# A transformer block's forward and backward on one core: the opening written out in order on all engines, with the first two head pairs run together

## The chip, the cores and the metric

The kernel runs on one core of a Trainium2 chip. The metric is the device time of one execution in microseconds; several runs of each kernel are made, and their median is given. The engines are named as in the profile: PE is TensorE, PEld its weight loads, DVE is VectorE, ACT is ScalarE, POOL is GpSimd and SP is SyncE, which issues DMAs.

## The reference: what is computed

A block with adaptive layer norms is computed together with its gradients. One row `c` gives six modulation rows through `silu(c) @ w_mod`; `sa, ca, ga` belong to the attention, `sb, cb, gb` to the MLP.

```python
h = _layernorm(x, axis=-1) * (1 + ca) + sa
x = x + ga * _A_ref(h, A_wqkv, A_wo)      # 32 heads of 16, softmax over all 2048 tokens
h = _layernorm(x, axis=-1) * (1 + cb) + sb
x = x + gb * _B_ref(h, B_w1, B_b1, B_w2, B_b2)   # relu(h @ w1 + b1)**2 @ w2 + b2
```

The sizes are 2048 tokens, width 512, MLP width 1792, all in bf16. The ten outputs are the block's result and the gradients of `A_x`, `A_wqkv`, `A_wo`, `w1`, `b1`, `w2`, `b2`, `c` and `w_mod` for a given `grad_out`.

## The kernel before

The program has a forward pass (`phase_fwd`, L265), a backward pass through the attention (`phase5`) and a last phase of weight gradients (`phase6`, L1392). Only the forward pass is touched.

**The attention loop (L331 to L375).** Heads are taken in quads of four (`g`, eight of them) and pairs (`jp`), queries in chunks of 512 (`qc`, four). A head pair of one query chunk is one turn `n` of the outer loop, 64 in all; in each turn the inner loop goes over the 16 key blocks `kb` of 128 tokens. One such step is called a unit. In a unit TensorE makes the scores of two heads (L349, two matmuls of 512 columns into one of two `st` banks; `QTm[j]` holds the queries of one head, with zeros in the rows of the others), ScalarE takes the exponential (L352, `pu`), and TensorE multiplies older `pu` tiles with the values (L314, eight matmuls of 17 columns, called PV). After the last key block VectorE normalises (L321, L322).

**What runs beside it.** While the first query chunk runs, a background generator (`gen_qkv`, L545) hands out single matmuls at a rate of 1.2 per unit: `gen_fm` (L519) projects Q or K of a quad for 512 tokens with four matmuls into a bank `pps` (two banks, shared by all of the opening), evicts them with VectorE (L535), stores them with SP (L536), and makes the token-major copy that the backward pass needs: a DMA transpose on SP (L538, `ev_tm`, three buffers), a copy (L540) and a store (L542) on GpSimd. From quad 3 on it also scales the weights (`wm_s`, L565) and pads the values (`vpad`, L583, L584) on GpSimd, for transposes that the backward pass needs. `load_q` (L293) fetches the queries of the next pair through GpSimd's queue half a pair ahead.

**The opening (`gen_open`, L389).** It loads `x`, the modulation weights and the projection weights through SP, computes the modulation columns (`silu_c`, `mod_cols`), and then, for each chunk of 512 tokens, the layer norm (`norm`: bn_stats and aggregates on VectorE, the power -0.5 on GpSimd, L443, the scaled rows `xhat` on VectorE or ScalarE), 16 transposes on TensorE (`turn`), the modulation into `xm1T` (L466 on VectorE and L469 on ScalarE, one each from the same bank), the K projection of quad 0, and the four value tiles (`values`, evicted in turn by VectorE and ScalarE, L479). The first chunk is done ahead of the loop, with the Q projection of quad 0, whose rows ScalarE copies out of PSUM (L531). Twenty matmuls on constants (L422, L430) keep TensorE busy meanwhile. The other three chunks are handed out piece by piece during the 16 units of head pair 0 (L356 to L361).

**What sets the order.** Under `tc.manual_schedule(engines={PE, SP})` (L160) TensorE and SP run in written order through the forward and backward pass. VectorE, ScalarE and GpSimd are ordered by a scheduler at build time, which may move an instruction ahead of others that were written earlier. [...]

Of the kernel before, what the change touches and what calls it, by code (L numbers as in the profile page):

```python
# [19 lines left out]
P = 128  # L20
DH = 16
EPS = 1e-5

# [81 lines left out]
class K:  # L105
# [71 lines left out]
    def phase0(self):  # L177
# [6 lines left out]
        nc.vector.tensor_copy(self.ident_f[:], self.ident[:])  # L184
# [80 lines left out]
    def phase_fwd(self):  # L265
# [21 lines left out]
        QTm = []  # L287
        for j in range(4):
            t = fw.tile([P, 512], BF16, name=f"QTm{j}")
            nc.vector.memset(t[:], 0.0)  # L290
            QTm.append(t)
# [36 lines left out]
        first = self.gen_open(Vaug, KT, QTm, stp)  # L328
        next(first)
        opening = [9 + DT + DT * 4] * (SC - 1) + [4 * DT + 1]  # L330
        for n, (qc, g, jp) in enumerate(order):  # L331
            if (qc, g, jp) == (1, 0, 0):
                bg.drain()
                self.close_qkv()
                self.open_mlp()
                bg.add(self.gen_weights())
# [3 lines left out]
            for kb in range(ST):  # L340
# [15 lines left out]
                if n == 0:  # L356
                    left = opening[kb // 4]
                    take = -(-left // (4 - kb % 4))
                    opening[kb // 4] -= take
                    for _ in range(take):  # L360
                        next(first)  # L361
                rate = (1.14 if qc else 1.2) if n or kb > 11 else 0
                room = int((SPAN - 2 - bg.plan(rate)) / PVT)
                while pend:
                    age = now - (pend[0][0][0] * ST + pend[0][0][4])
# [4 lines left out]
                if rate:  # L370
                    bg.step(rate)
# [17 lines left out]
    def gen_open(self, Vaug, KT, QTm, stp):  # L389
# [28 lines left out]
        nc.sync.dma_start(self.wmod[:, :, 2 * D:6 * D], wmod_v[:, :, 2 * D:6 * D])  # L418
        self.silu_c(ps)
        warm = ps.tile([P, 512], F32, name="pps")  # L420
        for _ in range(10):
            nc.tensor.matmul(warm[:], lhsT=self.ones_b[:], rhs=QTm[0][:], start=True, stop=True)  # L422
        for t in (1, 0):
            nc.vector.memset(self.wpad0[t][:], 0.0)
        nc.vector.memset(Vaug[:, :, :, DH:DH + 1], 1.0)
        nc.scalar.memzero(wpads[1][:])
        self.mod_cols(ps, (0, 1))
        warm = ps.tile([P, 512], F32, name="pps")
        for _ in range(10):
            nc.tensor.matmul(warm[:], lhsT=self.ones_b[:], rhs=QTm[0][:], start=True, stop=True)  # L430
# [55 lines left out]
        for k2 in range(0, DT, 2):  # L486
            for _ in turn(0, k2):
                pass
# [1156 lines left out]
```

## Time and profile before

| what | value |
|---|---|
| median of 7 runs | 2647.68 us (2635.89 to 2655.86) |
| profiled execution, its own time | 2647.97 us |
| its span | 2646.2 us |
| first exponential of the attention (L352) starts | 24.77 us |
| exponentials of head pair 0 | 24.77 to 61.9 us, 16 units |
| PE busy up to 65.2 us | 48.64 us |
| ACT busy up to 65.2 us | 36.69 us |
| DVE busy up to 65.2 us | 37.05 us |
| end of the forward attention | about 998 us |

In the rows of a timeline the columns are start and duration in us, the engine, the line, the operation, output and input tiles with sizes, the count of instructions merged into the row, and, in brackets, how long the engine had been idle and what released it. In rows of waits they are who waited for whom, the sum in us, how often, and the longest. In rows by stage they are the window, its length, busy us of each engine with its number of instructions, the granted clock of TensorE as a share of full speed (PEclk), the busy share of the DMA engines, and GB/s.

### The profile page before, as it was taken

How to read it: one execution, taken by the hardware profiler on the slowest of the kernel's cores; microseconds unless marked ns; L12 is line 12 of the kernel's file. 1: busy time of each engine (PE TensorE's matmuls, PEld its weight loads, DVE VectorE, ACT ScalarE, POOL GpSimd, SP SyncE). 2: the span in 40 equal slices, each digit the busy share in tenths (PEclk: the TensorE clock that was granted, in tenths of full speed). 3: DMA queues.
4: the chain of work that ended last, by engine and by line, in shares of the span. 5: the costliest groups of instructions: out<-in, count | busy, mean ns of one | idle time of the engine just before them, and what ended most of it. 6: DMA issues, size and time to landing. Idle time of an engine off the chain costs nothing. (4 is left out here: it accounts for less than half of the span.)

```text
span 2646.2 us, 76655 instructions
## 1 busy us (share of the span) xinstructions
PE 2484.4 (94%) x31000; PEld 1230.4 (46%) x31231; DVE 1767.1 (67%) x3653; ACT 2297.9 (87%) x3712; POOL 410.5 (16%) x678
## 2 busy tenths in 40 slices
PE   7999999999999999899999999999999999999997
PEld 3555555555555554753444444444444444443443
DVE  5222223423323344659999999999999999999867
ACT  5999999999999995318999999999999999999733
POOL 3344521310221131350000000000000000000041
PEclk9999999999999999899999999999999999999999
DMA  5488652440441245999999999999999999999986
GB/s 168 99 165 192 171 104 85 117 94 23 131 119 45 88 96 150 209 240 181 202 199 202 205 198 196 199 200 202 198 201 198 202 201 200 200 197 207 197 228 162
DMA packets 1197811, 441.16 MB, mean 167 GB/s; under 512 B 1134958, under 2 KB 1159024, under 8 KB 1197456
## 3 DMA queue, kind: packets, MB, share of 16 engines
q1 hardware_dynamic: 1167584, 347.42, 71.7%
q0 software_dynamic: 29872, 88.83, 11.5%
q8 instruction: 244, 4.00, 0.6%
q14 instruction: 111, 0.91, 0.1%
HBM read 83.30 MB, written 68.69 MB: 57 GB/s over the span
## 5 line engine op out<-in xcount | busy, mean ns | idle before, releaser
L1310 DVE TENSOR_TENSOR ds<-dp,pu 128x512 bf16<-128x512 f32 x2048 | 1242.2, 680 | 57.6 <-PE dp L1308 48.9
L1367 ACT ACTIVATE pu<-st 128x512 bf16<-128x512 f32 x2048 | 1083.0, 613 | 122.1 <-PE dp L1308 63.0
L352 ACT ACTIVATE pu<-st 128x1024 bf16<-128x1024 f32 x1024 | 944.5, 1072 | 18.3 <-PE st L349 15.7
L349 PE MATMUL st<-QTm,KTq 128*128 128x512 bf16 x1920 | 579.7, 377 | 31.2 <-ACT pu L352 7.2
L314 PEld LDWEIGHTS <-pu 128*128 128x128 bf16 x8192 | 347.4, 96 | 239.8 <-issue 4.9
L1287 PEld LDWEIGHTS <-dsT 128*128 128x128 bf16 x8192 | 245.0, 96 | 270.5 <-issue 205.8
L314 PE MATMUL accbank<-Vaug,pu 128*128 128x17 bf16 x8192 | 357.7, 171 | 7.0 <-ACT pu L352 0.3
L1308 PE MATMUL dp<-m,q 64*128 64x512 bf16 x1024 | 341.6, 386 | 0.7 <-DMA WmT<-WmT_d 0.7
L1308 PE MATMUL dp<-m,dOTq 64*128 64x512 bf16 x1024 | 337.2, 382 | 0.0
L1363 PE MATMUL st<-m,q 64*128 64x512 bf16 x1024 | 322.5, 385 | 7.7 <-ACT pu L1367 5.8
L1363 PE MATMUL st<-m,QTq 64*128 64x512 bf16 x1024 | 319.4, 381 | 6.2 <-ACT pu L1367 4.7
L349 PEld LDWEIGHTS <-KTq 128*128 128x128 bf16 x2048 | 193.5, 96 | 185.1 <-issue 132.0
L1418 POOL DMA_DIRECT2D O_tm<-O_d x2 | 1.8, 910 | 1317.9 <-PE accq L1287 1317.9
L1287 PE MATMUL accq<-Kg,dsT 128*128 128x16 bf16 x4096 | 149.3, 170 | 29.5 <-DMA dsT<-ds 29.0
L1287 PE MATMUL accq<-q,dsT 128*128 128x16 bf16 x4096 | 150.4, 170 | 27.3 <-DMA dsT<-ds 26.9
L1265 PE MATMUL acckv<-ds,q 128*16 128x512 bf16 x1024 | 155.5, 384 | 0.0
L1265 PE MATMUL acckv<-pu,q 128*16 128x512 bf16 x1024 | 155.5, 384 | 0.0
L1265 PE MATMUL acckv<-ds,Qg 128*16 128x512 bf16 x1024 | 154.4, 381 | 0.3 <-DVE ds L1310 0.2
L1265 PE MATMUL acckv<-pu,dOg 128*16 128x512 bf16 x1024 | 154.0, 381 | 0.0
L1328 ACT COPY dsT<-st 128x512 bf16<-128x512 bf16 x256 | 152.4, 595 | 1.2 <-PE st L1327 1.1
L321 DVE RECIPROCAL rl<-accbank 128x4 f32<-128x4 f32 x128 | 22.9, 179 | 149.2 <-PE accbank L314 149.1
L1363 PEld LDWEIGHTS <-q 64*128 64x128 bf16 x1024 | 58.2, 94 | 124.1 <-issue 104.8
(322 smaller groups left out, 2638.3 us busy)
## 6 DMA issues: line engine op xcount, KB each, us to landing
KTq<-KTq_d POOLq DMA_DIRECT2D x24, 512.0 KB, 3.8
duT_d<-auT POOLq DMA_DIRECT2D x4, 1792.0 KB, 8.7
aT_d<-rT POOLq DMA_DIRECT2D x4, 1792.0 KB, 12.9
KTq_d<-KTq SPq DMA_DIRECT2D x32, 128.0 KB, 2.0
QTq_d<-ev_fm SPq DMA_DIRECT2D x32, 128.0 KB, 3.0
VTq_d<-vT POOLq DMA_DIRECT2D x4, 1024.0 KB, 6.2
O_d<-O POOLq DMA_DIRECT2D x4, 1024.0 KB, 6.2
m<-KTq_d SPq DMA_DIRECT2D x32, 128.0 KB, 3.6
```

The lines of the kernel that those rows point to most:

```text
L314: nc.tensor.matmul(acc[:, a, sub, :], lhsT=pu[:, a, sub * P:(sub + 1) * P], rhs=Vaug[:, kb, h, :], start=(kb == 0 and a == 0 and sub == 0) ...
L321: nc.vector.reciprocal(self.rl[:, st0:st0 + 4, h], acc[:, a, :, DH])
L349: nc.tensor.matmul(stt[:, a, :], lhsT=KT[:, kb * P:(kb + 1) * P], rhs=QTm[2 * jp + a][:], start=True, stop=True)
L352: nc.scalar.activation(pu[:], stt[:], ACT.Exp, scale=self.scale)
L1265: nc.tensor.matmul(acckv[r:r + DH, :], lhsT=T[n][:, ib, col:col + DH], rhs=src[:, a, :], start=(ib == 0), stop=(ib == ST - 1))
L1287: nc.tensor.matmul(accq[:, ib, a, :], lhsT=dsT[:, (i * 2 + a) * 4 + sub, :], rhs=T["K"][:, 4 * c + sub, col:col + DH], start=(c == 0 and i ...
L1308: nc.tensor.matmul(dp[:], lhsT=T["dOT"][rd, ib * P:(ib + 1) * P], rhs=masked["VT"][2 * jp + a][rd, 512 * c:512 * (c + 1)], start=True, sto ...
L1310: nc.vector.tensor_tensor(dsg[:, i, a], dp[:], pu[:, a, :], ALU.mult)
L1328: nc.scalar.copy(dsT[:, 0:4, :], tp[:])
L1363: nc.tensor.matmul(stt[:], lhsT=T["QT"][rs, q], rhs=masked["KT"][2 * jp + a][rs, c0:c0 + 512], start=True, stop=True)
L1367: nc.scalar.activation(pu[:, a, :], stt[:], ACT.Exp, scale=self.scale)
L1418: nc.gpsimd.dma_start(O_tm[:, b, :], tm_v(self.O_d)[:, b, :])
```

## The change

The opening is put under `manual_schedule` for all five engines, so that it runs as it is written. Head pairs 0 and 1 (both of quad 0) are run together in 32 units: four key blocks of pair 0, the same four of pair 1, then the next four. Pair 0 has query tiles of its own (`QTo`), pair 1 uses `QTm[2]` and `QTm[3]`. In each period of 8 units the opening takes fixed pieces: one value tile in each of the first four units, a bank of transposes with its modulation in the fifth and sixth, the K projection of quad 0 in the seventh and four background matmuls in the eighth; in the last period the fifth and sixth units take background matmuls. Each bank of transposes is now evicted by one engine (two tiles by VectorE or two by ScalarE), and of four value tiles three go to VectorE. Q of quad 0 is evicted once by VectorE and copied from SBUF into the masked tiles.

The power is split in two for the first chunk, the statistics of a chunk are written one period ahead of its norm, and the constant matmuls number 12, 4, 4 and 2. The padded weights of quad 0 are copied by ScalarE instead of GpSimd. The token-major steps of the opening are collected in `late` and written one per unit from head pair 2. The `vpad` and `dgb_acc` memsets are written at the end of the opening.

From head pair 2 to the end of the first query chunk all engines but GpSimd keep the written order; GpSimd's is left to the scheduler. `wm_s` and `vpad` get a one-column operand that VectorE writes just ahead of them. From the second query chunk on only TensorE and SP have a written order, as before.

Of `gen_open` only the added lines are shown; the lines that they replace stand in the code above.

```diff
+ALL = {mybir.EngineType.PE, mybir.EngineType.SP, mybir.EngineType.DVE, mybir.EngineType.Activation, mybir.EngineType.Pool}
...
-        nc.vector.tensor_copy(self.ident_f[:], self.ident[:])
...
-        QTm = []
-        for j in range(4):
-            t = fw.tile([P, 512], BF16, name=f"QTm{j}")
-            nc.vector.memset(t[:], 0.0)
-            QTm.append(t)
+        QTm = [fw.tile([P, 512], BF16, name=f"QTm{j}") for j in range(4)]
...
-        first = self.gen_open(Vaug, KT, QTm, stp)
+        self.late = []
+        self.cur_g = 0
+        es = ExitStack()
+        es.enter_context(tc.manual_schedule(engines=ALL))
+        QTo = []
+        first = self.gen_open(Vaug, KT, QTm, QTo, stp, bg)
         next(first)
-        opening = [9 + DT + DT * 4] * (SC - 1) + [4 * DT + 1]
-        for n, (qc, g, jp) in enumerate(order):
+        accs = []
+        for n in range(2):
+            accb = accp.tile([P, 512], F32, name="accbank")
+            accs.append(accb[:, 0:8 * (DH + 1)].rearrange("p (a s e) -> p a s e", a=2, s=4))
+        units = [(n, 4 * s + k) for s in range(SC) for n in range(2) for k in range(4)]
+        for i, (n, kb) in enumerate(units):
+            if i == len(units) // 2:
+                bg.until(1)
+                load_q(*order[2])
+            stt = stp.tile([P, 2, 512], F32, name="st")
+            for a in range(2):
+                nc.tensor.matmul(stt[:, a, :], lhsT=KT[:, kb * P:(kb + 1) * P], rhs=(QTm[2 + a] if n else QTo[a])[:],
+                                 start=True, stop=True)
+            pu = pup.tile([P, 2, 512], BF16, name="pu")
+            nc.scalar.activation(pu[:], stt[:], ACT.Exp, scale=self.scale)
+            u = (n, 0, 0, n, kb, accs[n], pu)
+            next(first)
+            pend.extend((u, a, sub) for a in range(2) for sub in range(4))
+            while len(pend) > 16:
+                pv(pend.pop(0))
+        next(first)
+        es.close()
+        es.enter_context(tc.manual_schedule(engines=ALL - {mybir.EngineType.Pool}))
+        late, self.late = self.late, None
+        bg.until(-1)
+        KT = self.KT_next
+        for n, (qc, g, jp) in list(enumerate(order))[2:]:
...
                 bg.drain()
+                es.close()
...
-                if n == 0:
-                    left = opening[kb // 4]
-                    take = -(-left // (4 - kb % 4))
-                    opening[kb // 4] -= take
-                    for _ in range(take):
-                        next(first)
-                rate = (1.14 if qc else 1.2) if n or kb > 11 else 0
+                if late:
+                    late.pop(0)()
+                rate = 1.14 if qc else 1.2
                 room = int((SPAN - 2 - bg.plan(rate)) / PVT)
-                    age = now - (pend[0][0][0] * ST + pend[0][0][4])
+                    age = now - max(pend[0][0][0] * ST + pend[0][0][4], 2 * ST - 2)
...
-                if rate:
-                    bg.step(rate)
+                bg.step(rate)
...
-    def gen_open(self, Vaug, KT, QTm, stp):
+    def gen_open(self, Vaug, KT, QTm, QTo, stp, bg):
...
+        nc.gpsimd.memset(Vaug[:, :, :, DH:DH + 1], 1.0)
+        nc.vector.memset(QTm[0][:], 0.0)
         self.silu_c(ps)
...
+        QTo.extend(sa_.tile([P, 512], BF16, name=f"QTo{j}") for j in range(2))
+        for t in QTo + QTm[1:]:
+            nc.vector.memset(t[:], 0.0)
+        for t in self.wpad0 + wpads[::-1]:
+            nc.scalar.memzero(t[:])
+
+        def warm(n):
+            w = stp.tile([P, 2, 512], F32, name="st")
+            for _ in range(n):
+                nc.tensor.matmul(w[:, 0, :], lhsT=self.ones_b[:], rhs=QTm[0][:], start=True, stop=True)
+
+        warm(12)
...
+        def stat(st):
+            nc.vector.bn_stats(stats[:, st, :], x0[:, st, :])
+
+        def power(a, b):
+            for st in range(a, b):
                 nc.vector.bn_aggr(mv[:, st, :], stats[:, st, :])
...
+            nc.vector.tensor_scalar(ve[:, a:b], mv[:, a:b, 1], EPS, None, ALU.add)
+            nc.gpsimd.tensor_tensor(self.rstd1[:, a:b], ve[:, a:b], self.mhalf[:, 0:b - a], ALU.pow)
+
+        def norm(st):
+            nc.vector.tensor_scalar(xhat1[:, st, :], x0[:, st, :], mv[:, st, 0:1], self.rstd1[:, st:st + 1],
+                                    ALU.subtract, ALU.mult)
+
+        def store(s4):
+            nc.sync.dma_start(self.xhat1_d.rearrange("(st p) d -> p st d", p=P)[:, s4:s4 + 4, :], xhat1[:, s4:s4 + 4, :])
+
+        def turn(s4, k2, tp, ks=range(4)):
+            for k in ks:
+                for kt in range(2):
                     nc.tensor.transpose(tp[:, kt, k * P:(k + 1) * P],
                                         xhat1[:, s4 + k, (k2 + kt) * P:(k2 + kt + 1) * P], self.ident[:])
...
+
+        def scale(s4, k2, tp, act):
             for kt in range(k2, k2 + 2):
                 dst = xm1T[:, kt, s4 * P:s4 * P + 512]
...
+                if act:
+                    nc.scalar.activation(dst, tp[:, kt - k2, :], ACT.Identity, bias=self.mod_col(0)[:, kt:kt + 1],
+                                         scale=self.opcaT[:, kt:kt + 1])
+                else:
                     nc.vector.tensor_scalar(dst, tp[:, kt - k2, :], self.opcaT[:, kt:kt + 1], self.mod_col(0)[:, kt:kt + 1],
                                             ALU.mult, ALU.add)
...
...
+
+        def value(st):
+            pt = ps.tile([P, 512], F32, name="pps")
+            for kt in range(DT):
+                nc.tensor.matmul(pt[:], lhsT=xm1T[:, kt, st * P:(st + 1) * P], rhs=wq[:, kt, 2 * D:3 * D],
+                                 start=(kt == 0), stop=(kt == DT - 1))
+            (nc.scalar.copy if st % 4 == 3 else nc.vector.tensor_copy)(Vaug[:, st, :, 0:DH], pt[:].rearrange("p (h d) -> p h d", d=DH))
+
+        def pad0(t):
+            nc.scalar.copy(self.wpad0[t][:].rearrange("p k (j e) -> p k j e", e=32)[:, :, :, 0:DH],
+                           wq[:, :, t * D:t * D + 4 * DH].rearrange("p k (j d) -> p k j d", d=DH))
...
+        def fm(*a, **k):
+            for _ in self.gen_fm(ps, *a, **k):
+                pass
+
+        stat(0)
+        stat(1)
+        power(0, 2)
+        stat(2)
+        stat(3)
+        power(2, 4)
+        nc.vector.scalar_tensor_tensor(nmr[:, 0:1], mv[:, 0:1, 0], -1.0, self.rstd1[:, 0:1], ALU.mult, ALU.mult)
+        nc.scalar.activation(xhat1[:, 0, :], x0[:, 0, :], ACT.Identity, bias=nmr[:, 0:1], scale=self.rstd1[:, 0:1])
+        norm(1)
+        norm(2)
+        norm(3)
+        self.mod_cols(ps, (0, 1))
+        warm(4)
+        store(0)
+        pad0(1)
+        tps = [ps.tile([P, 2, 512], BF16, name="pps") for _ in range(2)]
+        for h in range(2):
+            turn(0, 2 * h, tps[h], (0, 1))
+        for h in range(2):
+            turn(0, 2 * h, tps[h], (2, 3))
+            scale(0, 2 * h, tps[h], h)
+        warm(4)
+        fm(1, 0, 0, dst=KT[:, 0:512])
+        pad0(0)
+        fm(0, 0, 0, masked=QTo + QTm[2:])
+        warm(2)
+        for st in range(4, 8):
+            stat(st)
+        power(4, 8)
+        nc.vector.tensor_copy(self.ident_f[:], self.ident[:])
         yield 0
...
+        for s4 in range(0, ST, 4):
+            n4 = s4 + 4
+            last = n4 == ST
+            value(s4)
             yield 0
...
+            value(s4 + 1)
+            if not last:
+                norm(n4)
+                norm(n4 + 1)
+            yield 0
+            value(s4 + 2)
+            if not last:
+                norm(n4 + 2)
+                norm(n4 + 3)
+                store(n4)
+            yield 0
+            value(s4 + 3)
+            if s4 == 0:
+                pad(0)
+            yield 0
+            for h in range(2):
+                if not last:
+                    tp = ps.tile([P, 2, 512], BF16, name="pps")
+                    turn(n4, 2 * h, tp)
+                    scale(n4, 2 * h, tp, h)
+                else:
+                    bg.take(DT)
+                if n4 + 4 < ST:
+                    stat(n4 + 4 + 2 * h)
+                    stat(n4 + 5 + 2 * h)
+                yield 0
+            if not last:
+                fm(1, 0, n4 * P, dst=KT[:, n4 * P:n4 * P + 512])
+            if n4 + 4 < ST:
+                power(n4 + 4, n4 + 8)
+            if s4 == 0:
+                pad(1)
+            yield 0
+            if not last:
+                bg.take(DT)
+            else:
+                for t in self.vpads:
+                    nc.gpsimd.memset(t[:], 0.0)
+                    nc.gpsimd.memset(t[:, :, :, DH:DH + 2], 1.0)
+                nc.gpsimd.memset(self.dgb_acc[:], 0.0)
+            yield 0
         self.close_pool("p1a")
         yield 0
...
-            yield 1
-        if masked:
-            for j in range(2):
-                nc.scalar.copy(masked[j][32 * j:32 * j + 32, :], pt[32 * j:32 * j + 32, :])
+            if kt < DT - 1:
+                yield 1
         if dst is None:
             ev = eb.tile([P, 512], BF16, name="ev_fm")
             dst = ev[:]
         nc.vector.tensor_copy(dst, pt[:])
+        if masked:
+            for j in range(4):
+                (nc.scalar.copy if j == 1 else nc.vector.tensor_copy)(masked[j][32 * j:32 * j + 32, :], ev[32 * j:32 * j + 32, :])
         nc.sync.dma_start((self.QTq_d, self.KTq_d)[t][g, :, s0:s0 + 512], dst)
-        tm = eb.tile([P, 4, 4, 32], BF16, name="ev_tm")
-        nc.sync.dma_start_transpose(tm[:].rearrange("p s j e -> p s (j e)"), dst)
-        tmc = eb.tile([P, 4, 4, DH], BF16, name="ev_tmc")
-        nc.gpsimd.tensor_copy(tmc[:], tm[:, :, :, 0:DH])
-        w = 4 * DH
-        nc.gpsimd.dma_start((self.qtm_d, self.ktm_d)[t][g, :, s0 // P * w:(s0 // P + 4) * w],
-                            tmc[:].rearrange("p s j d -> p (s j d)"))
+
+        def token_major():
+            tm = eb.tile([P, 4, 4, 32], BF16, name="ev_tm")
+            nc.sync.dma_start_transpose(tm[:].rearrange("p s j e -> p s (j e)"), dst)
+            tmc = eb.tile([P, 4, 4, DH], BF16, name="ev_tmc")
+            nc.gpsimd.tensor_copy(tmc[:], tm[:, :, :, 0:DH])
+            w = 4 * DH
+            nc.gpsimd.dma_start((self.qtm_d, self.ktm_d)[t][g, :, s0 // P * w:(s0 // P + 4) * w],
+                                tmc[:].rearrange("p s j d -> p (s j d)"))
+
+        if self.late is None:
+            token_major()
+        else:
+            self.late.append(token_major)
+        yield 1
...
-                nc.gpsimd.tensor_scalar(w[:], self.wq[:, g - 3, :], self.opcaT[:, g - 3:g - 2], 1.0, ALU.mult, ALU.mult)
+                sc = self.qkv_eb.tile([P, 1], F32, name="wm_c", bufs=2)
+                nc.vector.tensor_copy(sc[:], self.opcaT[:, g - 3:g - 2])
+                nc.gpsimd.tensor_scalar(w[:], self.wq[:, g - 3, :], sc[:], 1.0, ALU.mult, ALU.mult)
...
-            nc.gpsimd.tensor_copy(vp[:, :, 0:2, 0:DH], v[:, :, 2:4, :])
-            nc.gpsimd.tensor_copy(vp[:, :, 2:4, 0:DH], v[:, :, 0:2, :])
+            one = self.qkv_eb.tile([P, 1], F32, name="one", bufs=2)
+            nc.vector.memset(one[:], 1.0)
+            nc.gpsimd.tensor_scalar(vp[:, :, 0:2, 0:DH], v[:, :, 2:4, :], one[:], 1.0, ALU.mult, ALU.mult)
+            nc.gpsimd.tensor_scalar(vp[:, :, 2:4, 0:DH], v[:, :, 0:2, :], one[:], 1.0, ALU.mult, ALU.mult)
...
-        nc.gpsimd.memset(dgb[:], 0.0)
```

## The prediction

> **What bounds the kernel now.** I read the page first: busy shares, then the 40 slices.
>
> ```profile
> PE 2484.4 (94%) x31000; PEld 1230.4 (46%) x31231; DVE 1767.1 (67%) x3653; ACT 2297.9 (87%) x3712; POOL 410.5 (16%) x678
> ACT  5999999999999995318999999999999999999733
> ```
>
> ScalarE is full from the second slice (66 us each) to the end of the forward attention and only half full in the first. The change touches that first slice and the order of a few engines up to about 266 us; the built program's queues hold the same instructions in the same order on all engines after the first query chunk. So the question is how much earlier the full stretch starts.
>
> Next the exponentials of L352 alone, then all engines, by stage (window, length, busy us per engine, granted clock, DMA):
>
> ```profile
> core 0: us, ACT busy (x), PEclk, DMA share, GB/s
> 24.77:65.20 40.43, 19.31 (x20) 0.97 0.33 86
> 65.20:80.00 14.80, 14.68 (x17) 1.00 0.45 113
> ...
> core 0: us, PE busy (x) PEld busy (x) DVE busy (x) ACT busy (x) POOL busy (x), PEclk, DMA share, GB/s
> 24.77:65.20 40.43, 35.14 (x297) 18.46 (x301) 18.32 (x41) 27.37 (x34) 11.23 (x22) 0.97 0.33 86
> ```
>
> From 24.77 to 65.20 only 20 exponentials run; afterwards 17 in 14.80 us, without a gap. ScalarE's own order of time gives the pace:
>
> ```profile
> 24.77 1.02 ACT L352 ACTIVATE pu<-st 128x1024 bf16<-128x1024 f32 x1 [0.67 <-PE st L349]
> ...
> 60.89 1.02 ACT L352 ACTIVATE pu<-st 128x1024 bf16<-128x1024 f32 x1 [1.66 <-PE st L349]
> ...
> 62.27 38.23 ACT L352 ACTIVATE pu<-st 128x1024 bf16<-128x1024 f32 x41
> ```
>
> The 16 units of head pair 0 take 62.27 - 24.77 = 37.5 us, then 41 take 38.23, or 0.932 each. The 33rd exponential, the first of head pair 2, so starts at 62.27 + 16 x 0.932 = **77.2 us**. That is the number the change has to move. In the waits from 24 to 66 us:
>
> ```profile
> ACT pu L352 <- PE st L349: 11.7, 12, 1.7
> PE pps L476 <- ACT Vaug L479: 1.6, 3, 1.0
> PE pps L459 <- DVE Vaug L479: 1.0, 2, 0.8
> ```
>
> The exponentials wait for TensorE's scores, and TensorE, in written order, waits for evictions of the two projection banks that sit behind exponentials.
>
> **Part 1, the time to the first exponential (24.77 us now).** In the timeline of the first 25 us three things are late:
>
> ```profile
> 11.84 0.99 PE L232 MATMUL pps<-scT_b,wmod 128*128 128x1 bf16 x32 [5.18 <-DVE scT_b L216]
> ...
> 16.60 3.08 POOL L565 TENSOR_SCALAR wm_s<-wqkv,opcaT 128x1536 bf16<-128x1536 bf16 x2
> ...
> 19.65 1.04 POOL L443 TENSOR_TENSOR rstd<-ve,mhalf 128x4 f32<-128x4 f32 x1
> 20.72 0.42 DVE L451 TENSOR_SCALAR xhat<-x,mv,rstd 128x512 bf16<-128x512 bf16 x1 [1.91 <-POOL rstd L443]
> 21.05 0.54 DVE L466 TENSOR_SCALAR xm1T<-pps,opcaT,modT 128x512 bf16<-128x512 bf16 x1
> ```
>
> The scheduler put wm_s, needed much later, ahead of the second power on GpSimd, and VectorE, with the next tile's norm ahead of the last xm1T scale, waited for it. In written order neither stands there. I rebuild the chain with the rows' durations. x lands at 5.1 (first bn_stats). Five QTm/QTo memsets of 0.27 and the silu steps end about then. bn_stats 4 x 0.64, aggregates 2 x 0.30, two small adds: the second half's variance is out at 8.75. The power of 4 columns took 1.04; for 2 columns I know no row, so between 0.2 (the plain 4-column product, L219) and 1.04, and take 1.0, next to the power's own row: done 9.8. Norms 2 and 3 (0.41 each): 10.65. The modulation matmuls start with wmod at 7.8, so only their copies (0.4 to 0.6) follow: 11.3. The last transposes end 11.6 to 11.9, the two scales of the ScalarE bank (0.72 apart) at 13.3, with four warm matmuls beneath. K and Q projection, 8 matmuls 0.213 apart and 0.2 for the last result: 15.2. Q eviction 0.68, then three SBUF copies on VectorE beside one on ScalarE (a 32-row copy took 0.59): 16.5. First scores 0.6: exponential at 17.1, with 0.5 for a dozen hand-overs 17.6. wpad0's copies on ScalarE wait for weights; GpSimd had these at 10.2 and by 13.0, so they fit beneath.
>
> [...] The new opening has a stretch from about 8 to 13 us with only one-column matmuls, four warm ones and transposes. Here is the row, TensorE busy and granted clock per 2 us:
>
> ```profile
> 16.00:18.00 2.00, 1.86 (x19) 0.83 1.03 402
> 18.00:20.00 2.00, 0.81 (x3) 1.00 1.04 414
> 20.00:22.00 2.00, 0.36 (x2) 1.00 1.02 387
> 22.00:24.00 2.00, 1.34 (x6) 0.88 0.41 141
> 24.00:26.00 2.00, 1.98 (x12) 0.50 0.59 104
> ```
>
> The clock survives 4 us of nearly idle TensorE and then falls. [...] A fall did come here, so I take 0.7, nearer the row: first exponential at **18.3**, ends 17.1 and 21.4.
>
> **Part 2, 32 units instead of 16 beside the opening.** The work added to it is 16 units' scores (2 x 0.213), PV products (8 x 0.027) and exponentials, and the K and Q projections of quad 1 (5 x 0.85), all done after 62 us now. Matmuls of 512 columns start 0.213 apart (five in 1.24, the last one 0.38 long), PV products 0.027 (nine in 0.38, five in 0.27). Per period of 8 units TensorE has 8 x (0.43 + 0.21) + 4 values x 0.85 + 16 transposes x 0.055 + 2 projections x 0.85 = 11.1 us; ScalarE 8 x 0.92 + one value copy 0.5 + two scales 1.4 = 9.3; VectorE (3 value copies, 4 norms, 2 scales, 4 bn_stats, 2 evictions) 9.5. TensorE bounds, ScalarE no longer. Walking one period through the queues, with two score banks and two projection banks: units 0 to 3 cost TensorE 1.49 each and wait for nothing; in unit 6 the K projection's last two matmuls wait for the two ScalarE scales behind unit 5's exponential, 0.8 us. Period 11.9. The first lacks two PV groups (-0.4) but its third value waits for VectorE, where four bn_stats of the next tiles stand ahead of the first copy (+1.4): 12.9. The last has no transposes: 10.8. Sum 12.9 + 2 x 11.9 + 10.8 = 47.5. Before, the like sum was 7.7 a chunk (4 x 0.64 + 0.9 + 0.85 + 3.4) and it took about 9.4, so my walk may miss semaphore time; I add 3% of the sum, 1.4.
>
> Head pair 2 starts at 18.3 + 47.5 + 1.4 = **67.2 us**, 10.0 before 77.2. Four background matmuls fewer are done by then (20 against 24, 0.85 us); that costs nothing, for the filler finishes ahead of its drain.
>
> **Part 3, what is moved behind.** Ten token-major steps (DMA transpose on SP, copy and store on GpSimd) leave the opening and run one per unit from head pair 2, beside four regular ones; the vpad and dgb memsets go to the end of the opening on an idle GpSimd. The row for the transposes:
>
> ```profile
> L538 SPq DMA_TRANSPOSE ev_tm<-KTq x32: 1188/1196/2156, 23.2 to 256.5; - x32
> ...
> DMA to landing us min/median/max: 2.4/3.2/6.6
> ```
>
> SP spends 1.2 us on each; three ev_tm buffers, each held 3.2 + 0.4 (copy) + 0.3, allow one per 1.3 us. VectorE, now in written order, waits for them: it may write quad 2's first K chunk into quad 0's slot only when quad 0's transposes have read it, the last of which is ninth in SP's queue: 9 x 1.3 + 3.2 = 15 us after head pair 2 starts. It is wanted at unit 16.7, 15.4 us, and TensorE stops only one bank (3.5 us) later. Behind the waiting VectorE stand evictions and O's normalisation, and behind these TensorE. At 1.3 nothing stops. It is hidden by those 3.5 us; without that cover each 0.1 us of spacing costs 0.9. The loads of the next Q rows on GpSimd have half a head pair. The tiny VectorE operands of wm_s and vpad (some 30 of 0.06 to 0.17 us) lie on an engine that is 24% busy there; their effect is that the scheduler can no longer hoist that GpSimd work. The GpSimd form changes from a copy (0.45) to a scaled copy; the wm_s row (1.55 for 1536) makes 256 elements at most that: nothing, beneath GpSimd's idle time. ScalarE from head pair 2 holds only exponentials: no order to lose.
>
> **Sum.** The profiled execution was 2647.97 (span 2646.2), as good as the median 2647.68. 2647.7 - 10.0 = **2637.7**.
>
> **Rivals.**
> A, the in-order opening stalls as before: 9.4 / 7.7 = 1.22 applied to the 43.5 us of TensorE work is 53, and the start is 18.3 to 20: head pair 2 at 71.3 to 73, gain 4 to 6, **2642.5**. For it: every engine now has a written order, so each misplaced wait stops all; against: the banks that caused it now have one evicting engine each. 0.31.
> B, on the other side: the burst of transposes. If SP's transposes ran one after another, each its full landing time, the ninth would end at 9 x spacing; beyond (15.4 + 3.5) / 9 = 2.1 us it stops TensorE, at (18.9 + 10) / 9 = 3.2 the gain is gone, at 4.1 (between the 3.2 median and the 6.6 maximum) it costs 9 x 4.1 - 18.9 = 18: **2655.7**. Against: two transposes 2.2 us apart at 23 and 25 us both landed within about 5. 0.07.
> C, hardly any stall: start 17.1 and 43.5 of TensorE: 61, gain 16, **2631.5**. 0.10.
> Likeliest case, gain 8 to 13: 0.52.
>
> Against the bound of 0.3% (8 us, what a measurement can tell from no change): faster takes the likeliest case and C, 0.62; within 0.3% A, 0.31; slower B, 0.07. The range leaves out B and the edge of C, and allows a few us for the spread of the runs shown (2635.89 to 2655.86): 2631 to 2645.
>
> **What would show it.** First exponential at 17 to 19.5 (21 or more: the clock, visible as 0.50 granted between 10 and 18). Head pair 2's first exponential, the 33rd, at 65 to 69; ScalarE without a gap in the 16 units behind it, and no long wait of VectorE's K eviction on a DMA there (else B). wm_s and vpad on GpSimd no earlier than 100 us. Behind 270 us the same stage lengths as before. Wrong would be an opening with TensorE waiting at each value for VectorE, or a late stage that changes its length.

## The result and the profile after

| | before | after |
|---|---|---|
| median, us (runs) | 2645.3 (31) | 2632.05 (12; 2628.81 to 2644.51) |
| ratio, 95% interval | | 0.9955 (0.9943 to 0.9967) |
| profiled execution / span, us | 2647.97 / 2646.2 | 2628.81 / 2626.8 |
| first exponential, us | 24.77 | 16.71 |
| 33rd exponential (head pair 2), us | 77.22 | 64.68 |

The ratio is 11.9 us less (8.7 to 15.1). The forecast was 10.0 less, 2637.7, with a range of 2631 to 2645; the measured time lies within it, 1 us from its lower end. The two profiled spans differ by 19.4, and that is more than the change made: 12.5 lie ahead of head pair 2; the other 7 come from a stretch whose length varies by itself (shown with the first experiment).

The page of after, busy shares and ScalarE's slices. The first slice went from 5 tenths to 7; PE's busy time fell by 10 us on 3 more recorded instructions: no less work, but a higher granted clock, up to head pair 2 (4.3 us of it; 0.93 in before, 1.00 now) and in a later stretch (5.7, shown below).

```profile
PE 2474.6 (94%) x31003; PEld 1225.1 (47%) x31233; DVE 1770.4 (67%) x3681; ACT 2296.1 (87%) x3710; POOL 414.3 (16%) x676
...
ACT  7999999999999995319999999999999999999723
```

ScalarE's timeline of after, the rows that answer to those of before. The 33rd exponential is the first of the row with 28 in it; these run without a gap.

```profile
16.71 1.02 ACT L345 ACTIVATE pu<-st 128x1024 bf16<-128x1024 f32 x1 [0.46 <-PE st L342]
...
21.99 1.02 ACT L345 ACTIVATE pu<-st 128x1024 bf16<-128x1024 f32 x1 [1.67 <-PE st L342]
...
29.72 1.02 ACT L345 ACTIVATE pu<-st 128x1024 bf16<-128x1024 f32 x1 [0.47 <-PE st L342]
...
62.86 1.94 ACT L345 ACTIVATE pu<-st 128x1024 bf16<-128x1024 f32 x2 [0.47 <-PE accbank L310]
64.68 25.86 ACT L379 ACTIVATE pu<-st 128x1024 bf16<-128x1024 f32 x28
```

The four periods of eight units, by stage. TensorE is busy 11.35 of 12.08 us in the middle ones and bounds them; the first has four bn_stats too many on VectorE, the last no transposes.

```profile
16.71:29.72 13.01, 11.17 (x104) 6.03 (x105) 11.69 (x30) 10.00 (x12) 4.08 (x6) 1.00 0.68 252
29.72:41.80 12.08, 11.35 (x120) 6.38 (x121) 8.58 (x20) 9.89 (x11) 3.02 (x6) 1.00 0.19 66
41.80:53.88 12.08, 11.35 (x120) 6.38 (x121) 6.21 (x12) 9.89 (x11) 3.92 (x8) 1.00 0.22 73
53.88:64.68 10.80, 10.34 (x105) 5.63 (x106) 4.10 (x10) 8.44 (x9) 0.99 (x2) 1.00 0.11 38
```

The waits from 15 to 70 us:

```profile
ACT pu L345 <- PE st L342: 7.9, 16, 1.7
...
PE pps L606 <- ACT xm1T L488: 1.9, 6, 0.4
...
PE pps L497 <- DVE Vaug L499: 1.0, 1, 1.0
```

Exponentials waited for scores 11.7 us in before, in 16 units; now 7.9 in 32. The walk's two waits are both there: the K projection for ScalarE's scales, and in the first period the third value for VectorE.

### The profile page after: what moved, and what is told of

Its sections match the earlier page's. It is cut to its first block, busy times and chain, and to the rows that moved or that the text cites. A ratio compares the mean times of both kernels' runs of the same rounds, so it can differ in the third digit from the quotient of the medians.

```text
span 2626.8 us, 76691 instructions
## 1 busy us (share of the span) xinstructions
PE 2474.6 (94%) x31003; PEld 1225.1 (47%) x31233; DVE 1770.4 (67%) x3681; ACT 2296.1 (87%) x3710; POOL 414.3 (16%) x676
## 4 chain that ended last, share of the span: by engine, by line
PE 30%; DMA 25%; issue 2%; ACT 2%; POOL 0%; DVE 0%; SPq 0%; POOLq 0%; ACTq 0%; DVEq 0%
DMA dsT<-ds 23%; PE st L1455 11%; PE acckv L1357 6%; PE accq L1379 5%; PE dps L998 1%; ACT pu L1459 1%; PE dxhps L1536 1%; PE g3ps L1561 1%; PE dp L1400 1%; DMA dqT<-dq_t 1%; PE dps L947 1%; PE st L1419 1%; PE st L1368 1%; PE gps L1586 0%; DMA du_blk<-duT_d 0%
## 5 line engine op out<-in xcount | busy, mean ns | idle before, releaser
L379 ACT ACTIVATE pu<-st 128x1024 bf16<-128x1024 f32 x992 | 912.1, 1077 | 6.4 <-PE st L376 6.0
L376 PE MATMUL st<-QTm,KTq 128*128 128x512 bf16 x1859 | 561.7, 377 | 29.1 <-ACT pu L379 6.1
L376 PEld LDWEIGHTS <-KTq 128*128 128x128 bf16 x1984 | 188.1, 96 | 179.5 <-issue 125.6
L291 POOL DMA_DIRECT2D QTm<-QTq_d x124 | 63.1, 512 | 337.0 <-PE st L376 314.1
```

What stands on the lines that cost most here:

```text
L291: nc.gpsimd.dma_start(QTm[j][32 * j:32 * j + 32, :], self.QTq_d[g, 32 * j:32 * j + 32, 512 * qc:512 * (qc + 1)])
L376: nc.tensor.matmul(stt[:, a, :], lhsT=KT[:, kb * P:(kb + 1) * P], rhs=QTm[2 * jp + a][:], start=True, stop=True)
L379: nc.scalar.activation(pu[:], stt[:], ACT.Exp, scale=self.scale)
```

## The experiments

All times of stages below are from one profiled execution of each kernel. "Head pair 2" is the start of the 33rd exponential. A ratio is to the runs of before on the same chip; kernels without one have a single time.

| kernel | first exp. | head pair 2 | time, us | ratio to before |
|---|---|---|---|---|
| before | 24.77 | 77.22 | 2645.3 | |
| after | 16.71 | 64.68 | 2632.05 | 0.9955 (0.9943 to 0.9967) |
| one_pair | 16.70 | 69.95 | 2635.49 | 0.9968 (0.9954 to 0.9981) |
| sched_open | 21.87 | 70.45 | 2637.63 | 0.9990 (0.9978 to 1.0001) |
| mixed_evict | 16.96 | 65.54 | 2626.45 | one run |
| no_late | 16.70 | 75.88 | 2652.53 | one run |
| no_warm | 19.07 | 67.00 | 2633.45 | one run |
| stat_shift | 16.70 | 65.67 | 2632.90 | 0.9953 (0.9936 to 0.9970) |
| before_written | 28.96 | 107.13 | 2670.59 | one run |
| no_operand | 17.82 | 65.89 | 2636.86 | one run |
| swap_turns | 16.70 | 63.37 | 2632.46 | one run |
| swap_vaug | 18.05 | 64.72 | 2632.77 | 0.9939 (0.9921 to 0.9958) |

**Both kernels again, unchanged (after2, before2).** These give the spread of the stage times.

> The changed kernel once more, unchanged. Its first profile had the first exponential at 16.71 us and the 33rd (head pair 2) at 64.68, 12.5 before the 77.2 of the kernel before; but the stretch from the last PV product to the first ds of the backward pass was 192.1 us against 199.9, 7.8 more. My theory, that only the opening differs and those 7.8 are dips of TensorE's clock that come and go: 33rd exponential within 0.3 of 64.68, the stretch anywhere from 190 to 201. Rival, that the change also shortens that stretch: 192 again, within 1.

> The kernel before once more, unchanged. My theory: 33rd exponential within 0.3 of 77.2, the stretch from the last PV product to the first ds anywhere from 190 to 201. Rival, that this stretch is longer in the kernel before: 200 again, within 1.

After came back at 64.67; before at 78.32, 1.1 later than in its first profile, more than the 0.3 expected, because its first exponential came at 25.79. So a difference of 1 us against before is no finding; against after, 0.01 apart, it may be one. The stretch from the forward attention's last normalisation to the backward pass's first `ds` is another matter. By stage, before, after and before again:

```profile
997.50:1197.00 199.50, 180.86 (x1520) 112.60 (x1528) 111.05 (x455) 63.42 (x154) 80.45 (x113) 0.96 0.91 206
```

```profile
983.90:1175.70 191.80, 175.20 (x1520) 108.81 (x1529) 110.30 (x455) 63.44 (x154) 80.51 (x113) 1.00 0.94 214
```

```profile
1001.00:1196.30 195.30, 179.14 (x1532) 111.96 (x1530) 110.69 (x456) 63.49 (x154) 80.53 (x113) 0.97 0.88 210
```

The work is the same, but for a few matmul records, and the granted clock is 0.96, 1.00 and 0.97. Over the fourteen profiles here the stretch takes 191.1 to 194.3 us at 0.98 and more, and 195.1 to 200.1 at 0.96 and 0.97. Both texts of the opening stand on both sides: before_written, on the text of before, takes 194.0 at 0.98, and no_late, which has the changed opening, 200.1 at 0.97. So the length goes with the clock of that execution, and the 7.7 us that it adds to the difference of the two profiles are not counted. An effect of the change of a microsecond or two in it isn't excluded, and what made the clock dip was not tried.

**The two head pairs one after the other (one_pair).** The rest of the change stays.

```diff
-        units = [(n, 4 * s + k) for s in range(SC) for n in range(2) for k in range(4)]
+        units = [(0, kb) for kb in range(ST)]
...
             next(first)
+            next(first)
...
-        for n, (qc, g, jp) in list(enumerate(order))[2:]:
+        for n, (qc, g, jp) in list(enumerate(order))[1:]:
```

> The changed kernel with head pair 0 alone beside the opening, two pieces of the opening per unit, and head pair 1 in the main loop. My theory, that the start and the joint pairs are two gains: first exponential still at 16.7; TensorE's work beside 16 units is 3 x 8.56 + 7.66 = 33.3 us, with waits 36 to 38, then 16 exponentials at 0.932: the 33rd at 67.6 to 69.6, 3 to 5 later. Rival, that the whole gain is the earlier start and the joint pairs only move work about: the 33rd at 64.7 within 0.7.

Head pair 2 came 5.3 us later, a little beyond what the theory gave, and "all of it is the start" falls. ScalarE's timeline of one_pair has the old gaps back:

```profile
28.26 1.02 ACT L342 ACTIVATE pu<-st 128x1024 bf16<-128x1024 f32 x1 [1.86 <-PE st L339]
30.62 1.02 ACT L342 ACTIVATE pu<-st 128x1024 bf16<-128x1024 f32 x1 [1.33 <-PE st L339]
...
55.36 20.49 ACT L376 ACTIVATE pu<-st 128x1024 bf16<-128x1024 f32 x22
```

The sixteen units that carry the opening take 55.36 - 16.70 = 38.7 us here and took 37.5 in before. They carry more work here: 34 matmuls of the Q and K projections by the records against 17, with TensorE busy 35.5 us against 32.3; in before the rest follows beside exponentials without a gap. So behind the first exponential the written order and the one-engine banks make room for that work, but bring head pair 2 no nearer. What does is the second head pair, whose exponentials fill ScalarE while TensorE does the opening's work.

**The scheduler in the opening (sched_open).** The changed text, with the order of VectorE, ScalarE and GpSimd left to the scheduler as before.

```diff
-        es.enter_context(tc.manual_schedule(engines=ALL))
+        es.enter_context(tc.manual_schedule(engines={mybir.EngineType.PE, mybir.EngineType.SP}))
...
-        es.enter_context(tc.manual_schedule(engines=ALL - {mybir.EngineType.Pool}))
+        es.enter_context(tc.manual_schedule(engines={mybir.EngineType.PE, mybir.EngineType.SP}))
```

> The changed text, with VectorE, ScalarE and GpSimd left to the scheduler in the opening and the first query chunk; TensorE and SP in written order as in the kernel before. My theory, that the written order makes the earlier start: first exponential at 20 to 25, the 33rd at 70 to 77. Rival, that the new text alone does it: 16.7 and 64.7, within 1.

As expected: the first exponential at 21.87, and from there to head pair 2 48.6 us against 48.0. Of the 8.1 us at the start the changed text is thus worth 2.9 and the written order 5.2; behind the start the order is worth 0.6. Where the 5.2 are shows in the timeline of its start:

```profile
8.03 0.15 DVE L209 CAST cT<-pps 128x4 f32<-128x4 bf16 x1
...
9.08 1.83 POOL L588 MEMSET vpad<- 128x1024 bf16 x2
9.16 1.90 DVE L472 TENSOR_SCALAR xhat<-x,mv,rstd 128x512 bf16<-128x512 bf16 x1
...
12.07 0.99 PE L232 MATMUL pps<-scT_b,wmod 128*128 128x1 bf16 x32 [3.74 <-DVE scT_b L216]
```

VectorE does all the statistics ahead of `cT`, the first step of the modulation columns (3.49 in after), and a norm beside GpSimd's memset takes 1.90 instead of 0.40. The modulation matmuls start at 12.07 against 8.15, and TensorE, which had waited 3.74 us, then runs at 0.50 of its clock from 12 to 18 us. Before had the same late `scT_b` (11.84): its waits named the second power and the last scale, but those stood behind this one. The timing gives 0 to 5.8 us of gain over before where the trace gives 6.8; the missing microsecond or more has no place in the profile.

**Each bank evicted by both engines again (mixed_evict).**

```diff
-                if act:
+                if kt % 2 == 0:
...
-            (nc.scalar.copy if st % 4 == 3 else nc.vector.tensor_copy)(Vaug[:, st, :, 0:DH], pt[:].rearrange("p (h d) -> p h d", d=DH))
+            (nc.scalar.copy if st % 2 else nc.vector.tensor_copy)(Vaug[:, st, :, 0:DH], pt[:].rearrange("p (h d) -> p h d", d=DH))
```

> The changed kernel with each bank of transposes evicted by two engines again (one tile by ScalarE, one by VectorE), and the value tiles evicted in turn. My theory, that one engine per bank is worth about 1 us in each period of the opening: 33rd exponential at 67 to 68, period 13. Rival, that only order and joint pairs count: 64.7 within 0.5, period 12.1.

The rival was nearer: 0.9 us in all, 0.3 of it in the start. One engine for each bank, with the three-to-one split of the value tiles, is worth at most that here.

**The token-major steps inside the opening (no_late).**

```diff
-        self.late = []
+        self.late = None
...
-        late, self.late = self.late, None
+        late = []
```

> The changed kernel with the token-major steps written in the opening, each behind its projection, instead of one per unit behind it. My theory: GpSimd, in written order, then waits for a transpose ahead of the power of the next tiles, VectorE's norms wait, and the period grows by 1: 33rd exponential at 66 to 68. Rival, that the step is hidden and its deferral buys nothing: 64.7 within 0.5. The burst behind the opening is gone either way: if it cost anything, head pairs 2 and 3 take less than 29.8 us in this run than in the changed kernel.

Far later than expected: 75.88, 11.2 us behind after, nearly all of the gain gone. Waits from 16 to 76 us, GpSimd's timeline, and ScalarE's, all of no_late:

```profile
POOL ev_tmc L623 <- DMA ev_tm<-KTq: 40.8, 5, 15.4
ACT pu L345 <- PE st L342: 18.5, 18, 9.0
DVE xhat L472 <- POOL rstd L469: 10.1, 3, 8.6
PE pps L481 <- DVE Vaug L499: 9.1, 2, 8.0
```

```profile
25.57 0.40 POOL L623 COPY ev_tmc<-ev_tm 128x256 bf16<-128x256 bf16 x1 [15.39 <-DMA ev_tm<-KTq]
...
28.34 1.05 POOL L469 TENSOR_TENSOR rstd<-ve,mhalf 128x4 f32<-128x4 f32 x1
```

```profile
33.55 1.02 ACT L345 ACTIVATE pu<-st 128x1024 bf16<-128x1024 f32 x1 [9.05 <-PE st L342]
```

Read in order of cause: the first transpose is issued while the loads keep the DMA engines full (90% busy and more from 2.5 to 25 us) and lands 10.4 us after its issue (2.9 as a median when deferred); GpSimd, in written order, waits 15.4 us for it with the next power behind it; the power comes at 28.34 instead of 19.60; VectorE's norms wait 8.6 us for the power, with a value eviction behind them; TensorE waits 8.0 us for that bank; the exponential waits 9.0 us for the scores. The first period is 9.7 us longer for it, the later ones together 1.5.

**No constant matmuls behind the first twelve (no_warm).**

```diff
-        warm(4)
...
-        warm(4)
...
-        warm(2)
```

> The changed kernel with only the first 12 constant matmuls, not the 4, 4 and 2 later. [...] By the row of the kernel before, where the clock survived 4 us of little work: no loss, 16.4 to 16.8 and 64.4 to 64.8.

The row's range doesn't hold: the first exponential comes at 19.07, 2.4 us later than in after, and head pair 2 at 67.00, 2.3 later. The granted clock was 0.50 from 12 to 20 us, where after had 1.00. TensorE per 2 us, no_warm and then after:

```profile
10.00:12.00 2.00, 1.26 (x13) 0.75 1.11 349
12.00:14.00 2.00, 1.19 (x7) 0.50 1.10 347
14.00:16.00 2.00, 1.84 (x5) 0.50 1.12 356
```

```profile
10.00:12.00 2.00, 1.24 (x16) 1.00 1.10 347
12.00:14.00 2.00, 1.86 (x8) 1.00 1.10 349
14.00:16.00 2.00, 1.33 (x7) 1.00 1.11 352
```

**The statistics spread out (stat_shift).** Three of the four bn_stats and the power written behind the first value evictions, and the first two norms, which need that power, one unit later.

```diff
-        for st in range(4, 8):
-            stat(st)
-        power(4, 8)
+        stat(4)
...
             value(s4)
+            if s4 == 0:
+                stat(5)
+                stat(6)
             yield 0
             value(s4 + 1)
+            if s4 == 0:
+                stat(7)
+                power(4, 8)
```

> The changed kernel with the statistics of tiles 5 to 7 written behind the first two value tiles' evictions instead of ahead of them. My theory: the third value tile no longer waits for VectorE (1.04 us of wait and the rest of the gap), so the 33rd exponential comes at 63.3 to 63.9, 0.8 to 1.4 earlier. Rival, that the wait moves to the norms and the transposes behind them: 64.7 within 0.3, or later.

The rival was right: head pair 2 1.0 later. The gap at the fourth exponential went from 1.67 to 0.47 and came back at the sixth, in ScalarE's timeline of stat_shift:

```profile
25.56 1.02 ACT L345 ACTIVATE pu<-st 128x1024 bf16<-128x1024 f32 x1 [2.26 <-PE st L342]
```

The norms need the power, and the power all four statistics. VectorE has as much to do in either order, so what moves is the exponential that pays.

**Written order on the text of before (before_written).**

```diff
+        es = ExitStack()
+        es.enter_context(tc.manual_schedule(engines=ALL))
         first = self.gen_open(Vaug, KT, QTm, stp)
...
+            if n == 1:
+                es.close()
+                es.enter_context(tc.manual_schedule(engines=ALL - {mybir.EngineType.Pool}))
```

> The kernel before with its own text, but all five engines in written order in head pair 0, and all but GpSimd to the end of the first query chunk. My theory, that the order is only as good as the text: wm_s no longer stands ahead of the power, so the first exponential comes at 17.5 to 20, but GpSimd's 8 weight copies (4.5 us), vpad memsets (2.2) and token-major copies, which wait for transposes, now stand ahead of the next power, VectorE waits, and the 33rd exponential is no earlier than 77. Rival, that written order alone is the gain: 33rd at 72 or less.

Right that it is slower, wrong in the first exponential, which came at 28.96 and not near 18; head pair 2 is 30 us later than in before. GpSimd's timeline:

```profile
14.02 3.07 POOL L572 TENSOR_SCALAR wm_s<-wqkv,opcaT 128x1536 bf16<-128x1536 bf16 x2 [9.67 <-DMA wqkv<-in_A_wqkv_dram]
17.06 1.06 POOL L450 TENSOR_TENSOR rstd<-ve,mhalf 128x4 f32<-128x4 f32 x1
...
27.99 0.40 POOL L547 COPY ev_tmc<-ev_tm 128x256 bf16<-128x256 bf16 x1 [9.18 <-DMA ev_tm<-KTq]
...
38.52 1.05 POOL L450 TENSOR_TENSOR rstd<-ve,mhalf 128x4 f32<-128x4 f32 x1
```

`wm_s` lies in the text that GpSimd's scheduler still orders, behind the written part, and it was put ahead of that part's first power all the same; then the token-major copies hold the next power, as in no_late. An order written on a text that isn't arranged for it is much worse than the scheduler's.

**`wm_s` and `vpad` without the VectorE operand (no_operand).**

```diff
-                nc.gpsimd.tensor_scalar(w[:], self.wq[:, g - 3, :], sc[:], 1.0, ALU.mult, ALU.mult)
+                nc.gpsimd.tensor_scalar(w[:], self.wq[:, g - 3, :], self.opcaT[:, g - 3:g - 2], 1.0, ALU.mult, ALU.mult)
```

(`vpad` likewise in its old form, and the operands' two VectorE lines dropped.)

> The changed kernel with wm_s and the vpad copies in their old form, without the column that VectorE writes. The build puts the two first wm_s (1.55 us each) on GpSimd between the second and the third power. My theory now: both start when the V weights land, about 12.5 us, and end at 16, ahead of the third power at 19.6, so nothing is late: first exponential 16.7, the 33rd 64.7, within 0.3. Rival, that this is what held up the opening before and does so again: the third power 1 us or more later, the 33rd exponential at 66 or later.

The scheduler did hoist `wm_s` into the opening, and it cost 1.2 us. The rival came near in its numbers (the third power at 20.81 instead of 19.60, head pair 2 at 65.89) but not in its path: `wm_s` didn't hold the power, ahead of which GpSimd was idle for 3.8 us. In the timeline of no_operand from 10 to 19 us:

```profile
13.91 3.07 POOL L654 TENSOR_SCALAR wm_s<-wqkv,opcaT 128x1536 bf16<-128x1536 bf16 x2 [3.73 <-DMA wqkv<-in_A_wqkv_dram]
...
15.62 1.50 DVE L616 COPY QTo<-ev_fm 32x512 bf16<-32x512 bf16 x1
17.15 0.59 DVE L616 COPY QTm<-ev_fm 32x512 bf16<-32x512 bf16 x2
```

The copy of 32 rows that the first scores wait for takes 0.28 us in after; here it takes 1.50 and ends at 17.12, just behind GpSimd's `wm_s` at 16.98. The norm of 1.90 in sched_open, up to 11.06, likewise ran beside a GpSimd memset that ended at 10.91. Not every VectorE instruction beside that `wm_s` was longer: its two evictions before the copy took 0.69 each, as in after. What makes the copy long isn't shown; no other form of it was tried.

**The order of the two banks (swap_turns).** In each period ScalarE's bank first, VectorE's second, so that the K projection doesn't wait for ScalarE behind an exponential.

```diff
-                    turn(n4, 2 * h, tp)
-                    scale(n4, 2 * h, tp, h)
+                    turn(n4, 2 - 2 * h, tp)
+                    scale(n4, 2 - 2 * h, tp, 1 - h)
```

> The changed kernel with the two banks of transposes of a period in the other order: the one that ScalarE scales in the fifth unit, the one that VectorE scales in the sixth. If the 0.8 us that the K projection waits for ScalarE's scales is what the walk said, three periods get shorter by 0.6 to 0.8 each: period 11.3 to 11.5, 33rd exponential at 62.3 to 63. Rival, that the wait is only exchanged, since VectorE's bn_stats now stand ahead of its scales: 64.7 within 0.4.

Head pair 2 at 63.37, 1.3 earlier; a middle period takes 11.65 instead of 12.08. The wait on ScalarE there shrank and one of 0.5 for VectorE's scale took its place. That a gain of 1.3 us is in the time isn't shown: the single run can't tell it.

**That, with the values' ones written by VectorE (swap_vaug).** GpSimd's strided memset of 2.26 us (0.88 to 3.1) stands ahead of the identity that starts the modulation chain; VectorE does it instead.

```diff
-        nc.gpsimd.memset(Vaug[:, :, :, DH:DH + 1], 1.0)
         nc.vector.memset(QTm[0][:], 0.0)
+        nc.vector.memset(Vaug[:, :, :, DH:DH + 1], 1.0)
```

> As swap_turns, and with the ones of Vaug written by VectorE, in its wait for the first transpose, instead of by GpSimd ahead of the identity. The GpSimd memset took 2.26 us (on VectorE in the kernel before 0.48) and the identity, the silu steps and the statistics came 0.9 later for it. Theory: first exponential 15.8 to 16.0, and the 33rd 0.8 earlier than swap_turns. Rival, that wmod's landing at 7.9 and the clock set the start: 16.5 to 16.7 still.

A miss: 18.05, later and not earlier. VectorE's timeline, and TensorE in three stretches between which its clock changed:

```profile
3.12 0.48 DVE L442 MEMSET Vaug<- 128x512 bf16 x1 [1.69 <-issue]
...
5.96 1.22 DVE L463 BATCH_NORM_STATS2 stats<-x 128x6 f32<-128x512 bf16 x2
```

```profile
7.72:11.13 3.41, 2.25 (x41) 1.00 1.10 352
11.13:14.55 3.42, 3.42 (x18) 0.50 1.10 348
14.55:17.96 3.41, 2.74 (x13) 1.00 1.08 386
```

The memset itself takes 0.48, but VectorE was idle for 1.69 us ahead of it (1.72 ahead of the same memset in before), for nothing that the profile shows, so the statistics start at 5.96 as in after (5.99); and the clock fell to 0.50 with the same number of warm matmuls with which it was 1.00 in after. The first twelve ran earlier, up to 7.56 instead of 8.31; whether that made the clock fall isn't shown. Its ratio, 0.9939, has an interval that overlaps that of after; it isn't shown to be better.

## Why the prediction was right, point by point

**The sum.** 10.0 us were forecast, 11.9 (8.7 to 15.1) measured, 12.5 in the trace up to head pair 2. Both parts had the right sign and were somewhat too small: the start 8.1 (forecast 6.5), the periods 52.5 to 48.0, that is 4.5 (forecast 52.4 to 48.9, 3.5). Both marks came just ahead of the ranges given for them, 16.71 (17.1 to 21.4) and 64.68 (65 to 69). That 2632.05 lies as near as it does to rival C's 2631.5 is chance in part: the forecast started from 2647.7, and the median of all 31 runs of before is 2.4 less.

**The start, 18.3 forecast, 16.71 measured.** The mis-sized terms are the two allowances: 0.7 for the clock, which stayed at 1.00, and 0.5 for hand-overs. The chain itself, 17.1, fits well, in part by luck, for its errors cancel. The timeline of after:

```profile
0.88 2.26 POOL L441 MEMSET Vaug<- 128x512 bf16 x1
...
5.99 1.22 DVE L463 BATCH_NORM_STATS2 stats<-x 128x6 f32<-128x512 bf16 x2
...
9.32 0.86 POOL L469 TENSOR_TENSOR rstd<-ve,mhalf 128x2 f32<-128x2 f32 x1 [0.88 <-DVE nmr L521]
...
12.95 1.91 PE L606 MATMUL pps<-xm1T,wpad 128*128 128x512 bf16 x8
...
15.63 0.28 DVE L616 COPY QTo<-ev_fm 32x512 bf16<-32x512 bf16 x1
```

The statistics began 0.9 later than 5.1, behind the silu chain that the GpSimd memset delays: a cost that I hadn't listed. The two-column power took 0.86 (0.73 the first), 1.0 taken. The scales ended at 13.5 (13.3), but the projection had begun at 12.95 on the tiles that were ready, and 8 matmuls took 1.91; I had started it behind both. Nor had I seen that the first scores need only two of the four copies, this one of 0.28 and ScalarE's of 0.62 beside it.

**What made the start late in before** was named only in part. `wm_s`, the power and the last scale were read rightly as the last waits; sched_open shows that without them the modulation chain behind the statistics still makes 21.87. The rows of before showed it (5.18 us idle ahead of the modulation matmuls); my list of three late things had it first, and the explanation named only the other two.

**The clock.** The row gave nothing lost. With the warm matmuls nothing was: the granted clock was 1.00 from 6 to 24 us. Without the last ten it fell to 0.50 and the start came 2.4 us later, so those ten are worth 2.4 us here. No run shows the 0.7 that the forecast holds for the clock, nor the 3.8 that lies between its 17.6 and its end of 21.4; the runs show no loss in after and 2.4 in no_warm. The ten don't make it safe: in swap_vaug, which has them too, the clock was 0.50 from 11.13 to 14.55. The row itself reads otherwise in stretches of 3.41 us; its clock rose at 16.68, fell at 23.50 and rose at 26.92. TensorE of before:

```profile
16.68:20.09 3.41, 1.99 (x21) 1.00 1.02 408
20.09:23.50 3.41, 1.24 (x5) 1.00 0.73 273
23.50:26.92 3.42, 3.36 (x14) 0.50 0.60 135
```

The 4 us with little work, from 18 to 22, lie in the first two of these, beside busy time that brings them to 1.99 and 1.24 us. That the clock stayed at 1.00 through them therefore says nothing of a whole stretch with little work: behind 6.45 to 9.86, with 0.21 us busy, it was 0.50. How much busy time goes with a full clock isn't shown: behind 1.99 us it was 1.00 here, behind 2.25 in swap_vaug 0.50.

**The periods.** Walked at 12.9, 11.9, 11.9 and 10.8, measured 13.01, 12.08, 12.08 and 10.80, so 0.47 of the 1.4 allowed. Sums by engine and a walk through two pairs of banks were enough. The measured 64.68 lies between the forecast's 67.2 and rival C, hardly a stall, at 61; rival A, the opening stalling as before, with head pair 2 at 71 to 73, didn't come.

**The token-major steps: the outcome right, the reason not seen.** I priced only what their deferral might cost and found nothing. That held: the transposes ran 1.29 apart, as in SP's timeline,

```profile
76.30 5.15 SPq L621 DMA_TRANSPOSE ev_tm<-KTq  x4
```

and in VectorE's waits of 64.7 to 95 us no DMA appears; the 32 exponentials from head pair 2 on take 29.95 us to the start of the next with the burst and 29.96 in no_late without it. So rival B fell. But the deferral buys 11.2 us, the largest single effect in the study, and the prediction had no line for it. The waits of before from 24 to 66 us held a sign of it:

```profile
POOL ev_tmc L540 <- DMA ev_tm<-KTq: 15.9, 3, 8.9
```

There these waits cost nothing: the scheduler had GpSimd's order, and the long ones stand behind the last power, which started at 32.6 us. The cost follows from asking, for each engine newly in written order, what it would wait for with the power queued behind.

**The operands** were put at nothing for their time and to keep `wm_s` where it is written. The second held and is worth 1.2 us, though through a VectorE copy that took 1.2 us longer and not through a late power.

**The parts don't add.** Undone one at a time they cost 11.2 (deferral), 5.8 (written order), 5.3 (joint pairs), 2.3 (warm matmuls), 1.2 (operands) and 0.9 (one engine per bank), 26.7 in all, against a gain of 12.5: the likely reading is that the deferral and the arranged text pay for what written order would otherwise cost, which before_written has at 30.

## What to carry to other kernels

When an engine is put in written order, go along its queue and ask of each instruction what it waits for and what stands behind it: a copy that waits for a DMA must not stand ahead of a step on the path, and moving those is part of the price of the order (here 11 us, more than the order brings). Where a prologue is bound by TensorE, a second stream of independent units beside it can bring more than better evictions (here 5.3 us against 0.9). Don't credit a change with a stretch that it doesn't touch before the same kernel was profiled twice.

## What had not been expected of the hardware

A VectorE copy of 32 x 512 took 1.50 us instead of 0.28, up to 0.14 us past the end of a GpSimd instruction, and a norm 1.90 instead of 0.40 beside a GpSimd memset. GpSimd's memset of 512 strided elements took 2.26 us where VectorE's took 0.48. A transpose issued beside bulk loads took up to 10.4 us to land, 2.9 as a median later. And the same stretch behind the forward attention took 191 to 200 us from one execution to the next, at a granted clock of 1.00 to 0.96. Around the opening the changes of that clock lay 3.41 us or twice that apart, within 0.01 (11.13 and 14.55 in swap_vaug; 9.86, 16.68, 23.50 and 26.92 in before).
